# Layer 1 of a mixture of experts on blocks of 768 tokens instead of 384, with its layer 2 right behind, and weight preparation stepping inside layer 1

## The chip, the cores and the metric

The kernel runs on one core of a Trainium2 chip. TensorE (PE) multiplies, VectorE (DVE) and ScalarE (ACT) work on tiles, GpSimd (POOL) does a few special operations, and SyncE (SP) issues nearly all DMAs. The metric is device microseconds of one execution, the median of several runs. Lower is better.

## The reference

Three stages follow one another, all in float32:

```
attention, 4 x 8 heads x 576 positions x 64, window of 64      -> x, 2304 tokens x 512
mixture 1: P = Sinkhorn(softmax(x @ w_gate)), 8 experts
           x1 = sum over e of P[:, e] * (relu(x @ w1[e]) @ w2[e])   (512 -> 1024 -> 512, every token)
mixture 2: each token goes to one expert (capacity 288, greedy by logit)
           out[t] = relu(x1[t] @ v1[e]) @ v2[e]
```

Mixture 1 is dense: each of the eight experts works on all 2304 tokens.

## The kernel before, in words

Each float32 operand is split into two float16 parts, high and low (xh and xl, hh and hl, and so on), and a product is the sum of three matmuls: high by high, high by low, low by high. Partial sums stay in PSUM in float32.

Tokens come in 18 tiles of 128, and TB = 3 tiles make a block of BT = 384 (HB = 192 is half a block, NB = 6 blocks). Expert 0 of mixture 1 is computed beside the attention (line 761). For experts 1 to 7, layer 1 goes by Strassen's scheme (layer1s): the tokens of a block are two halves, the 1024 hidden columns two halves, the 512 inputs two halves, and seven products p1 to p7 take the place of eight. One product is six matmuls of 128 x 192 (line 853). A unit is the seven products for one f of four; it makes hidden chunks f and 4 + f of the block. Some of the operands are combinations of token halves: they are kept as T (th, tl, made by strassen_x) or written over one quarter of x (T1).

ACT copies a product out of PSUM (sa, sb, sc: lines 865, 877, 886), because the next product adds into the same bank; DVE adds the other product; then emit_evac (lines 734, 735) makes hh with a ReLU on ACT and hl on DVE. ACT and DVE take their instructions in order.

Layer 2 (line 931) takes a tile of 128 tokens at a time: 24 matmuls of 512 columns, then one DVE instruction adds the scaled result to acc (line 947). It is a generator that stops four times a tile, so a step is six matmuls.

stream() writes the order of PE's queue by hand. Unit u's products stand at slots 7u + 0, 1, 3, 5, 6, 9, 11; units overlap so that most slots are filled. A free slot takes a step of layer 2: before slot 7 of the block before the last (head), later of the last block (tail). run(e, bs) streams the units of the blocks bs; the first run of an expert has two blocks and no tail. hbuf holds two blocks of hidden values, one per block by turns.

The weights are prepared in the background. weights_all goes through a list of jobs: load 2 MB of float32 weights into raw by four DMAs, scale them by a power of two found from their norm (sum_scale: squares on ACT and DVE, a small matmul with ones on PE at line 293, a few DVE instructions), and split them into high and low. For mixture 2 and for w2 the parts go to DRAM from four small buffers, st2k (ACT line 336, DVE line 338, SP's DMA); for w1 they go to the seven Strassen combinations in SBUF, and this part waits until layer 1 of the expert before is done. bg.tick(level, dt) moves the background's clock on by dt and steps each task that is due and whose level is at least the tick's; a task says how long it wants to wait until its next step. Weights are level 0, as are the last expert's row tiles (finish_all) and gate weights (held_weights). load_w2, which brings the next w2 from DRAM into w2b, is level 1, so it steps at every tick. Layer 2 ticks after each three matmuls (level 0, dt 1). Layer 1 ticks at every third slot, at level 1, dt 2.3. bg.until(name) ticks until a task is done, with no matmul in between.

For the last expert, the last two blocks are held back: their gate logits are computed from the hidden values (held_logits), and the rest of layer 2 runs beside the routing of mixture 2.

Of the kernel before, what the change touches and what calls it, by code (L numbers as in the profile page):

```python
# [172 lines left out]
def body(ctx, tc, q, k, v, wg1, w11, w12, wg2, w21, w22, out):  # L173
# [43 lines left out]
    lg = base.tile([128, NT, E], F32, name="lg")  # L217
    P = base.tile([128, NT, E], F32, name="P")
    SE = base.tile([128, E, NT], F32, name="SE")
    lg2 = base.tile([128, NT, E], F32, name="lg2")  # L220
    lgh = base.tile([128, 2 * TB, E], F32, name="lgh")
    ident = base.tile([128, 128], F32, name="ident")
    wgs = base.tile([128, DC, 2 * E], F16, name="wgs")
    wginv = base.tile([128, 1], F32, name="wginv")
# [51 lines left out]
    def sum_scale(buf, inv, sc, key=None):  # L276


        mp = small.tile([128, 8], F32, name="np8")
        e = []  # L280
        for c in range(0, 8, 2):
            kd = [(key, c // 2)] if key else []
            a = yield Rq("ACT", 0.8, kd, wait=1.3)
            junk = st2k() if "pool" in rc else acc[:, NT - 2].bitcast(F16)
            s0, s1 = [buf[:, x * 512:(x + 1) * 512] for x in (c, c + 1)]
            A.activation(junk[:, 0:512], s0, AF.Square, accum_out=mp[:, c:c + 1])  # L286
            d = yield Rq("DVE", 0.77, kd, wait=0)
            V.scalar_tensor_tensor(junk[:, 512:1024], s1, 1.0, s1, op0=OP.mult, op1=OP.mult, accum_out=mp[:, c + 1:c + 2])
            e += [a.end, d.end]
        m1 = small.tile([128, 1], F32, name="m1")  # L290
        p = yield Rq("PE", 0.2, e, "psb", wait=2.3)
        pt = psb.tile([128, 512], F32, name="pb")
        PE.matmul(pt[:, 0:8], rc["ones"], mp, start=True, stop=True)
        d = yield Rq("DVE", 0.9, [p.end])
        V.tensor_reduce(m1, pt[:, 0:8], AX.X, OP.add)
        norm_pow2(m1, sc, inv)
        fl.release("psb", p.idx, d.start + 0.3)
        rc["sct"] = d.end
# [474 lines left out]
        if i == NT - 1:  # L773
            bg.done.add(("l2x", 0))

    def strassen_x(b):

        c0, c1 = b * BT, b * BT + HB

        def part(x, d, c):  # L780
            return x[:, d:d + 2, c:c + HB]
# [40 lines left out]
        fl.at["T", b] = e  # L822

    def strassen_all():
        for b in range(NB):
            while ("l1b", b) not in bg.done or "T" not in rc or ("lg", b * TB + TB - 1) not in bg.done:
                yield IDLE
            yield from strassen_x(b)
            bg.done.add(("T", b))

    def bq(name, b):
        c0, c1 = b * BT, b * BT + HB
        if name in ("B11", "T1"):
            c = c0 if name == "B11" else c1
            return [x[:, 0:2, c:c + HB] for x in (xh, xl)]
        if name in ("B21", "B22"):
            c = c0 if name == "B21" else c1
            return [x[:, 2:4, c:c + HB] for x in (xh, xl)]
        n = {"T2": 0, "T3": 1, "T4": 2}[name]
        return [t[:, n, :, b * HB:(b + 1) * HB] for t in rc["T"]]  # L840

    def layer1s(e, b):

        hh, hl = hbuf[b % 2]
        sp = rc["spool"]

        def prod(bank, a, x, f, start):
            fs = slice(f * 128, f * 128 + 128)
            aq, xq = wq[a], bq(x, b)
            n = 0  # L850
            for c in range(2):
                for wi, xi in ((0, 0), (0, 1), (1, 0)):
                    PE.matmul(bank[:, 0:HB], aq[wi][:, c, fs], xq[xi][:, c], start=(start and n == 0), stop=(n == 5),  # L853
                              skip_group_check=True)
                    n += 1

        lo, hi = slice(0, HB), slice(HB, BT)
        nf = FC // 2
        s = {}

        def p1(f):
            s["b1", f] = ps1.tile([128, BT], F32, name="p1")
            prod(s["b1", f], "A11", "B11", f, True)
            s["a", f] = sp.tile([128, HB], F32, name="sa")
            A.activation(s["a", f], s["b1", f][:, 0:HB], AF.Copy)

        def p2(f):
            b3 = psb.tile([128, 512], F32, name="pb")
            prod(b3, "A12", "B21", f, True)
            t = s["a", f]  # L870
            V.tensor_tensor(t, b3[:, 0:HB], t, OP.add)  # L871
            emit_evac(hh, hl, f, lo, t)

        def p6(f):
            prod(s["b1", f], "S2", "T2", f, False)
            s["b", f] = sp.tile([128, HB], F32, name="sb")
            A.activation(s["b", f], s["b1", f][:, 0:HB], AF.Copy)  # L877

        def p5(f):
            s["b2", f] = psb.tile([128, 512], F32, name="pb")  # L880
            prod(s["b2", f], "S1", "T1", f, True)

        def p7(f):
            prod(s["b1", f], "S3", "T3", f, False)
            t = s["c", f] = sp.tile([128, HB], F32, name="sc")
            A.activation(t, s["b1", f][:, 0:HB], AF.Copy)  # L886
            V.tensor_tensor(t, s["b2", f][:, 0:HB], t, OP.add)

        def p4(f):
            prod(s["b1", f], "A22", "T4", f, False)  # L890
            emit_evac(hh, hl, nf + f, lo, s["b1", f][:, 0:HB])
            emit_evac(hh, hl, nf + f, hi, s["c", f])

        def p3(f):
            prod(s["b2", f], "S4", "B22", f, False)
            t = s["b", f]
            V.tensor_tensor(t, s["b2", f][:, 0:HB], t, OP.add)  # L897
            emit_evac(hh, hl, f, hi, t)

        return [((0, p1, f), (1, p2, f), (3, p6, f), (5, p5, f), (6, p7, f), (9, p4, f), (11, p3, f)) for f in range(nf)]  # L900

    def stream(units, head, tail):

        at = {}
        for u, unit in enumerate(units):
            for t, fn, f in unit:
                at[7 * u + t] = (fn, f)
        last = max(at)
        for t in range(last + 1):
            if t in at:  # L910
                fn, f = at[t]
                fn(f)
                if t % 3 == 2:
                    bg.tick(1, 2.3)
            else:
                g = head if t < 7 else tail
                if g:
                    next(g, None)
        for _ in head:
            pass  # L920

    def layer2(e, b, out=None):
        hh, hl = hbuf[(1 if b == NB - 2 else 0) if e == 0 else b % 2]
        for j in range(TB):
            i = b * TB + j
            p = ps2.tile([128, DM], F32, name="p2")
            js = slice(j * 128, j * 128 + 128)
            n = 0
            for f in range(FC):
                for h, wi in ((hh, 0), (hh, 1), (hl, 0)):  # L930
                    PE.matmul(p, h[:, f, js], w2v[wi][:, f], start=(n == 0), stop=(n == 3 * FC - 1))  # L931
                    n += 1
                    if n in (3, 6, 9, 12, 15, 18, 21):
                        bg.tick()
                    if n in (6, 12, 18):
                        yield
# [564 lines left out]

    def drain(g, keep=0):

        n = 12 - g[1] - keep
        for _ in range(n):
            next(g[0], None)
        g[1] += n

    def run(e, bs):

        drain(pend[0], 2)
        us = []
        for b in bs:
            us += layer1s(e, b)
        g = [layer2(e, bs[0] - 1), 3] if bs[0] else None
        stream(us, pend[0][0], g and g[0])
        pend[0] = g

    rc["spool"] = mid.enter_context(tc.tile_pool(name="spool", bufs=2))
    for e in range(1, E):  # L1520
        bg.until(("w1", e))
        if e == 1:
            bg.until(("T", 1))
        if e == E - 1:
            bg.start("lgh", held_gate(), 1)
        run(e, [0, 1])
        bg.until(("w2", e), "gates")
        scales(e)
        if e == E - 1:
            bg.start("finish", finish_all())  # L1530
            bg.start("w2h", held_weights())
        pend[0] = [layer2(e, 0), 0]
        for b in range(2, NB):
            if e == 1:
                bg.until(("T", b))
            run(e, [b])
        bg.done.add(("l1", e))
        if e < E - 1:
            drain(pend[0])
            pend[0] = [layer2(e, NB - 1), 0]  # L1540
            drain(pend[0], 3)
            bg.done.add(("l2", e))
    bg.until("weights", "lgh", "w2h")
    mid.close()
    rc["rpool"] = late.enter_context(tc.tile_pool(name="rpool", bufs=1))
# [5 lines left out]

    def rest():
        n = len(finals)
        for g in (pend[0][0], layer2(E - 1, NB - 1)):
            for _ in g:
                while n < len(finals):
                    for _ in to_rows(finals[n], n % 2):
                        pass
                    n += 1


    second()
# [23 lines left out]
```

## Time and profile before

| | |
|---|---|
| median of 3 runs | 1899.92 us (1897.87 to 1900.22) |
| the profiled execution | 1898.91 us |
| its span, first to last instruction | 1897.1 us |
| mean granted clock of PE | 0.987 of full speed |
| layer-1 matmuls of experts 1 to 7, first and last start | 317.4 and 1566.6 us |

The page gives for each engine the time in which it had an instruction running. Matmuls are pipelined, so the length of one matmul (246 ns for 192 columns) says less than the distance from one to the next. A wait is put down to the instruction that released it.

### The profile page before, as it was taken

The page shows a single profiled execution, that of the slowest core. Times are in us where ns is not written, and L with a number is a line of the kernel's source. Part 1 is how long each engine was busy: PE and PEld are TensorE (multiplying, and loading weights), DVE is VectorE, ACT ScalarE, POOL GpSimd, SP SyncE. Part 2 cuts the span into 40 slices and gives each one's busy share as a digit, 9 for nine tenths or more (in the row PEclk, how much of TensorE's full clock was granted, in tenths as well). Part 3 has the DMA queues.
Part 4 walks back from the last instruction along what each step waited for, and adds up shares of the span by engine and source line. Part 5 has one row for each costly group of instructions (what it writes and reads, how often), then busy time and mean ns, then how long its engine had stood idle before and what let it go on. Part 6 is the DMA issues. An engine that isn't in the chain of part 4 may idle for free.

```text
span 1897.1 us, 40554 instructions
## 1 busy us (share of the span) xinstructions
PE 1830.4 (96%) x16103; PEld 1311.0 (69%) x16103; DVE 1235.9 (65%) x3768; ACT 886.0 (47%) x2439; POOL 116.2 (6%) x160
## 2 busy tenths in 40 slices
PE   6999999999999999999999999999999998899987
PEld 5777556767767677667766867667687774677766
DVE  7877955654666766676667666766757767575630
ACT  6776334533555545555554555555534443122222
POOL 0000000000000000000000000000000103233231
PEclk8999999999999999999999999999999999899999
DMA  7663022220333234334252343234231111545360
GB/s 182 124 162 69 13 77 89 90 90 1 112 126 119 90 105 164 115 109 134 90 178 68 112 155 114 95 115 148 90 106 27 36 30 57 187 166 178 123 220 26
DMA packets 172798, 203.38 MB, mean 107 GB/s; under 512 B 83000, under 2 KB 130104, under 8 KB 168512
## 3 DMA queue, kind: packets, MB, share of 16 engines
q1 hardware_dynamic: 164928, 157.78, 27.2%
q0 software_dynamic: 7680, 43.02, 6.5%
q8 instruction: 126, 2.06, 0.4%
q14 instruction: 64, 0.52, 0.1%
HBM read 143.05 MB, written 57.71 MB: 106 GB/s over the span
## 4 chain that ended last, share of the span: by engine, by line
PE 80%; DVE 10%; DMA 4%; ACT 3%; issue 1%; another core or an unknown queue 1%; POOL 0%; SPq 0%; POOLq 0%; ACTq 0%; DVEq 0%
PE p L931 31%; PE p L853 17%; PE pb L853 12%; PE p L1309 4%; PE p L761 4%; PE p L1295 3%; DMA raw<-in_moe_w_dram 1%; PE pb L1140 1%; DVE st2k L338 1%; PE pb L621 1%; DMA w2scr<-st2k 1%; PE pb L608 1%; DVE oh L1221 1%; PE pb L979 1%; DMA ws<-st2k 1%
## 5 line engine op out<-in xcount | busy, mean ns | idle before, releaser
L931 PE MATMUL p<-w2b,hh 128*128 128x512 f16 x2304 | 685.7, 379 | 0.0
L931 PE MATMUL p<-w2b,hl 128*128 128x512 f16 x1152 | 436.6, 379 | 0.0
L931 PEld LDWEIGHTS <-hh 128*128 128x128 f16 x2304 | 221.8, 99 | 217.4
L853 PEld LDWEIGHTS <-w1b 128*128 128x128 f16 x4032 | 340.3, 98 | 23.0 <-issue 4.2
L853 PEld LDWEIGHTS <-w1x 128*128 128x128 f16 x3024 | 256.3, 98 | 19.7 <-issue 5.4
L853 PE MATMUL p<-th,w1x 128*128 128x192 f16 x1344 | 221.2, 246 | 3.6 <-ACT sb L877 2.1
L853 PE MATMUL pb<-xh,w1b 128*128 128x192 f16 x1344 | 221.2, 246 | 0.0
L931 PEld LDWEIGHTS <-hl 128*128 128x128 f16 x1152 | 112.6, 98 | 135.8 <-issue 0.9
L853 PE MATMUL pb<-xl,w1b 128*128 128x192 f16 x672 | 165.3, 246 | 0.0
L853 PE MATMUL p<-tl,w1x 128*128 128x192 f16 x672 | 165.3, 246 | 0.0
L338 DVE SCALAR_TENSOR_TENSOR st2k<-raw,wsc,st2k 128x512 f16<-128x512 f32 x128 | 92.1, 749 | 50.4 <-ACT st2k L336 50.1
L336 ACT ACTIVATE st2k<-raw,wsc 128x512 f16<-128x512 f32 x128 | 86.9, 713 | 69.4 <-DMA ws<-st2k 58.4
L947 DVE SCALAR_TENSOR_TENSOR acc<-p,SE,acc 128x512 f32<-128x512 f32 x126 | 94.0, 746 | 37.1 <-PE p L931 36.7
L734 ACT ACTIVATE hh<-sb 128x192 f16<-128x192 f32 x168 | 61.0, 363 | 112.7 <-DVE sb L897 112.7
L853 PE MATMUL p<-th,w1b 128*128 128x192 f16 x672 | 110.5, 246 | 3.1 <-ACT sc L886 2.9
L734 ACT ACTIVATE hh<-sa 128x192 f16<-128x192 f32 x168 | 60.9, 363 | 107.4 <-DVE sa L871 107.4
L853 PE MATMUL pb<-xh,w1x 128*128 128x192 f16 x672 | 110.6, 246 | 0.0
L853 PE MATMUL p<-xh,w1b 128*128 128x192 f16 x672 | 110.6, 246 | 0.0
L286 ACT ACTIVATE st2k<-raw 128x512 f16<-128x512 f32 x116 | 72.3, 625 | 78.5 <-DMA raw<-in_moe_w_dram 48.0
L996 POOL TENSOR_TENSOR st2k<-tmp,st2k 128x512 f16<-128x512 f32 x18 | 24.4, 1353 | 1372.1 <-ACT tmp L994 1350.8
L871 DVE TENSOR_TENSOR sa<-pb,sa 128x192 f32<-128x192 f32 x168 | 60.0, 357 | 72.7 <-PE pb L853 70.2
L735 DVE SCALAR_TENSOR_TENSOR hl<-sa,hh 128x192 f16<-128x192 f32 x168 | 60.3, 359 | 72.1 <-ACT hh L734 72.1
(303 smaller groups left out, 3245.4 us busy)
## 6 DMA issues: line engine op xcount, KB each, us to landing
raw<-in_moe_w_dram SPq DMA_DIRECT2D x128, 512.0 KB, 5.2
ws<-st2k SPq DMA_DIRECT2D x128, 256.0 KB, 4.5
w2b<-w2scr SPq DMA_DIRECT2D x28, 512.0 KB, 7.3
w2scr<-st2k SPq DMA_DIRECT2D x48, 256.0 KB, 4.6
xrows<-st2k SPq DMA_DIRECT2D x18, 257.0 KB, 3.1
vs<-in_v_dram SPq DMA_DIRECT2D x35, 128.0 KB, 3.5
ldq<-in_q_dram SPq DMA_DIRECT2D x16, 256.0 KB, 4.0
ldk<-in_k_dram SPq DMA_DIRECT2D x16, 256.0 KB, 4.4
```

What stands on the lines that cost most here:

```text
L286: A.activation(junk[:, 0:512], s0, AF.Square, accum_out=mp[:, c:c + 1])
L336: A.activation(hi, src, AF.Copy, scale=sc)
L338: V.scalar_tensor_tensor(lo, src, sc, hi, op0=OP.mult, op1=OP.subtract)
L734: A.activation(hh[:, f, cols], src, AF.Relu)
L735: V.scalar_tensor_tensor(hl[:, f, cols], src, 0.0, hh[:, f, cols], op0=OP.max, op1=OP.subtract)
L761: PE.matmul(p[:, 0:w], w1v[wi][:, c, fs], x[:, c, ts], start=(n == 0), stop=(n == 3 * DC - 1))
L853: PE.matmul(bank[:, 0:HB], aq[wi][:, c, fs], xq[xi][:, c], start=(start and n == 0), stop=(n == 5), skip_group_check=True)
L871: V.tensor_tensor(t, b3[:, 0:HB], t, OP.add)
L931: PE.matmul(p, h[:, f, js], w2v[wi][:, f], start=(n == 0), stop=(n == 3 * FC - 1))
L947: V.scalar_tensor_tensor(acc[:, i], p, SE[:, e, i:i + 1], acc[:, i], op0=OP.mult, op1=OP.add)
L1295: PE.matmul(p[:, 0:CAP], wv1[f // 4][w][:, c, fs], xt[:, x * DC + c], start=(n == 0), stop=(n == 3 * DC - 1))
L1309: PE.matmul(p[:, 0:CAP], wv2[f // 4][w][:, f % 4, dsl], x[:, f], start=(n == 0), stop=(n == 3 * FC - 1))
```

## The change

A block of layer 1 for experts 1 to 7 is now SB = 768 tokens (NS = 3): the two halves of Strassen's scheme are two blocks of 384, so a product is six matmuls of 128 x 384, and the copies and ReLUs of ACT and the DVE operations are 384 wide. The first half writes hbuf[0], the second hbuf[1]. T holds the same amount, in halves of 384. The layer 2 that fills the last free slots of a run, and the stretch behind it, is that of the same block (24 steps, six tiles); it reads hidden chunks 3 and 7 last, which the last unit writes.

Layer 1 ticks after every product, with dt 1.5, at level 0 for even slots and 1 for odd ones. The norm product asks to wait 4.0 instead of 2.3. The copies sa and sc have one buffer instead of two. lg2 and lgh are now views of lg.

```diff
@@ body
+    SB = 2 * BT
+    NS = N // SB
...
-    lg2 = base.tile([128, NT, E], F32, name="lg2")
-    lgh = base.tile([128, 2 * TB, E], F32, name="lgh")
+    lg2 = lg
+    lgh = lg2[:, NT - 2 * TB:]
@@ sum_scale
-        p = yield Rq("PE", 0.2, e, "psb", wait=2.3)
+        p = yield Rq("PE", 0.2, e, "psb", wait=4.0)
@@ strassen_x
-    def strassen_x(b):
-        c0, c1 = b * BT, b * BT + HB
+    def strassen_x(b, part_of):
+        o = part_of * HB
+        c0, c1 = b * SB + o, b * SB + BT + o
...
-        bs = slice(b * HB, (b + 1) * HB)
+        bs = slice(b * BT + o, b * BT + o + HB)
@@ strassen_all
-        for b in range(NB):
-            while ("l1b", b) not in bg.done or "T" not in rc or ("lg", b * TB + TB - 1) not in bg.done:
+        for b in range(NS):
+            while ("l1b", 2 * b + 1) not in bg.done or "T" not in rc or ("lg", (b + 1) * 2 * TB - 1) not in bg.done:
                 yield IDLE
-            yield from strassen_x(b)
+            for x in range(2):
+                yield from strassen_x(b, x)
@@ layer1s
-        hh, hl = hbuf[b % 2]
+        lo, hi = hbuf
...
-                    PE.matmul(bank[:, 0:HB], aq[wi][:, c, fs], xq[xi][:, c], start=(start and n == 0), stop=(n == 5),
+                    PE.matmul(bank[:, 0:BT], aq[wi][:, c, fs], xq[xi][:, c], start=(start and n == 0), stop=(n == 5),
...
-            s["a", f] = sp.tile([128, HB], F32, name="sa")
+            s["a", f] = sp.tile([128, BT], F32, name="sa", bufs=1)
...
-            emit_evac(hh, hl, nf + f, lo, s["b1", f][:, 0:HB])
-            emit_evac(hh, hl, nf + f, hi, s["c", f])
+            emit_evac(*lo, nf + f, every, s["b1", f][:, 0:BT])
+            emit_evac(*hi, nf + f, every, s["c", f])
@@ stream
-                if t % 3 == 2:
-                    bg.tick(1, 2.3)
+                bg.tick(t % 2, 1.5)
@@ layer2
-        hh, hl = hbuf[(1 if b == NB - 2 else 0) if e == 0 else b % 2]
-        for j in range(TB):
-            i = b * TB + j
+        bufs = hbuf if e else [hbuf[1 if b == NB - 2 else 0]]
+        fs = range(FC) if e == 0 else (0, 1, 2, 4, 5, 6, 3, 7)
+        for j in range(TB * len(bufs)):
+            i = b * TB * len(bufs) + j
...
-            for f in range(FC):
+            for f in fs:
@@ the experts
-    def run(e, bs):
-        drain(pend[0], 2)
-        us = []
-        for b in bs:
-            us += layer1s(e, b)
-        g = [layer2(e, bs[0] - 1), 3] if bs[0] else None
-        stream(us, pend[0][0], g and g[0])
-        pend[0] = g
+    def second_layer(e, b):
+        if b == 0:
+            bg.until(("w2", e), "gates")
+            scales(e)
+            if e == E - 1:
+                bg.start("finish", finish_all())
+                bg.start("w2h", held_weights())
+        yield from layer2(e, b)
...
-        run(e, [0, 1])
...
-        for b in range(2, NB):
+        for b in range(NS):
             if e == 1:
                 bg.until(("T", b))
-            run(e, [b])
+            drain(pend[0], 2)
+            us = layer1s(e, b)
+            g = [second_layer(e, b), 3, 24]
+            stream(us, pend[0][0], g[0])
+            pend[0] = g
         bg.done.add(("l1", e))
         if e < E - 1:
-            drain(pend[0])
-            pend[0] = [layer2(e, NB - 1), 0]
-            drain(pend[0], 3)
-            bg.done.add(("l2", e))
+            drain(pend[0], 2)
```

## Rows read from the trace of the kernel before

**Rows 1.** The page, part 1: busy us (share), instructions of each engine.

```profile
PE 1830.4 (96%) x16103; PEld 1311.0 (69%) x16103; DVE 1235.9 (65%) x3768; ACT 886.0 (47%) x2439; POOL 116.2 (6%) x160
```

**Rows 2.** Stretches: length, PE, PEld, DVE, ACT, POOL busy, PE clock, DMA share, GB/s.

```profile
700.00:800.00 100.00, 99.58 (x816) 71.02 (x814) 64.63 (x173) 52.35 (x143) 0.00 (x0) 1.00 0.37 125
1600.00:1700.00 100.00, 85.38 (x941) 63.03 (x941) 63.43 (x250) 21.52 (x43) 27.76 (x28) 0.88 0.47 162
```

**Rows 3.** Line 853, weight loads: count, min/median/max ns, first and last start.

```profile
L853 PEld LDWEIGHTS <-w1b x4032: 95/98/181, 317.2 to 1564.8; 128*128 128x128 f16 x192
L853 PEld LDWEIGHTS <-w1x x3024: 95/98/181, 319.5 to 1566.6; 128*128 128x128 f16 x189
```

**Rows 4.** Timeline of DVE, 512 to 524: start, us, line, operation, [idle before].

```profile
512.61 0.36 DVE L871 TENSOR_TENSOR sa<-pb,sa 128x192 f32<-128x192 f32 x1 [0.34 <-PE pb L853]
...
523.01 0.36 DVE L871 TENSOR_TENSOR sa<-pb,sa 128x192 f32<-128x192 f32 x1 [0.34 <-PE pb L853]
```

**Rows 5.** The chain that ended last, long pieces: start, us, matmuls.

```profile
257.67 15.60 PE p L761 x96
...
828.58 24.61 PE p L931 x114
```

**Rows 6.** Waits of PE: for whom, us in total, times, longest.

```profile
PE p L853 <- ACT sc L886: 2.9, 7, 0.4
PE p L853 <- ACT sb L877: 2.1, 4, 0.7
PE p L853 <- ACT sa L865: 1.3, 2, 0.9
PE pb L293 <- DVE st2k L288: 0.6, 1, 0.6
```

**Rows 7.** Groups of ACT by form: count, busy us, mean ns, idle before.

```profile
L336 ACT ACTIVATE st2k<-raw,wsc 128x512 f16<-128x512 f32 x128 | 86.9, 713 | 69.4 <-DMA ws<-st2k 58.4 <-DVE wsc L307 10.9
L286 ACT ACTIVATE st2k<-raw 128x512 f16<-128x512 f32 x116 | 72.3, 625 | 78.5 <-DMA raw<-in_moe_w_dram 48.0 <-DMA ws<-st2k 20.1 <-DMA w2scr<-st2k 4.4
L741 ACT ACTIVATE hh<-p 128x384 f16<-128x384 f32 x40 | 19.4, 485 | 36.3 <-PE p L761 36.1
```

**Rows 8.** Groups of DVE by form, the same columns.

```profile
L338 DVE SCALAR_TENSOR_TENSOR st2k<-raw,wsc,st2k 128x512 f16<-128x512 f32 x128 | 92.1, 749 | 50.4 <-ACT st2k L336 50.1
L743 DVE SCALAR_TENSOR_TENSOR hl<-p,hh 128x384 f16<-128x384 f32 x40 | 22.1, 554 | 15.9 <-ACT hh L741 15.9
```

**Rows 9.** Timeline of ACT, 808 to 813 us.

```profile
811.53 0.63 ACT L286 ACTIVATE st2k<-raw 128x512 f16<-128x512 f32 x1 [1.04 <-DMA w2scr<-st2k]
...
812.16 0.31 ACT L877 ACTIVATE sb<-p 128x192 f32<-128x192 f32 x1
```

**Rows 10.** The page, part 6: DMA issues, KB each, us to landing.

```profile
raw<-in_moe_w_dram SPq DMA_DIRECT2D x128, 512.0 KB, 5.2
ws<-st2k SPq DMA_DIRECT2D x128, 256.0 KB, 4.5
w2b<-w2scr SPq DMA_DIRECT2D x28, 512.0 KB, 7.3
```

**Rows 11.** Timeline of SP's DMA queue, 499 to 530 us.

```profile
501.71 3.22 SPq L463 DMA_DIRECT2D w2b<-w2scr  x4
529.56 0.56 SPq L422 DMA_DIRECT2D ws<-st2k  x1
```

**Rows 12.** Line 801, the operands T, columns as in rows 3.

```profile
L801 DVE TENSOR_TENSOR tl<-st2k,th x18: 546/553/560, 191.7 to 299.9; 128x384 f16<-128x384 f32 x18
```

**Rows 13.** Timeline of DVE, 1535 to 1600 us.

```profile
1572.14 0.23 DVE L1078 TENSOR_SCALAR tri<-jpr 128x128 f16<-128x128 f32 x1 [2.15 <-POOL jpr L1077]
```

**Rows 14.** Timeline of POOL, 1562 to 1570 us.

```profile
1562.08 0.38 POOL L1023 PARTITION_ALL_REDUCE mm<-m  x1 [9.87 <-DVE m L1021]
1569.78 1.15 POOL L996 TENSOR_TENSOR st2k<-tmp,st2k 128x512 f16<-128x512 f32 x1 [7.32 <-issue]
```

**Rows 15.** Timeline of PE, 1600 to 1612 us.

```profile
1605.57 0.97 PE L1229 MATMUL pb<-rh,oh 128*96 128x6 f16 x18 [1.50 <-DVE rh L1225]
```

More of the change, by code (lines that the diff above doesn't have):

```diff
@@ L821, in strassen_x @@
         fl.release("st2k", i21, e)
-        fl.at["T", b] = e
     def strassen_all():
-        for b in range(NB):
-            while ("l1b", b) not in bg.done or "T" not in rc or ("lg", b * TB + TB - 1) not in bg.done:
+        for b in range(NS):
+            while ("l1b", 2 * b + 1) not in bg.done or "T" not in rc or ("lg", (b + 1) * 2 * TB - 1) not in bg.done:
                 yield IDLE
-            yield from strassen_x(b)
+            for x in range(2):
+                yield from strassen_x(b, x)
             bg.done.add(("T", b))
     def bq(name, b):
-        c0, c1 = b * BT, b * BT + HB
+        c0, c1 = b * SB, b * SB + BT
         if name in ("B11", "T1"):
             c = c0 if name == "B11" else c1
-            return [x[:, 0:2, c:c + HB] for x in (xh, xl)]
+            return [x[:, 0:2, c:c + BT] for x in (xh, xl)]
         if name in ("B21", "B22"):
             c = c0 if name == "B21" else c1
-            return [x[:, 2:4, c:c + HB] for x in (xh, xl)]
+            return [x[:, 2:4, c:c + BT] for x in (xh, xl)]
         n = {"T2": 0, "T3": 1, "T4": 2}[name]
-        return [t[:, n, :, b * HB:(b + 1) * HB] for t in rc["T"]]
+        return [t[:, n, :, b * BT:(b + 1) * BT] for t in rc["T"]]
     def layer1s(e, b):
-        hh, hl = hbuf[b % 2]
+        lo, hi = hbuf
         sp = rc["spool"]
@@ L852, in prod @@
                 for wi, xi in ((0, 0), (0, 1), (1, 0)):
-                    PE.matmul(bank[:, 0:HB], aq[wi][:, c, fs], xq[xi][:, c], start=(start and n == 0), stop=(n == 5),
+                    PE.matmul(bank[:, 0:BT], aq[wi][:, c, fs], xq[xi][:, c], start=(start and n == 0), stop=(n == 5),
                               skip_group_check=True)
                     n += 1
-        lo, hi = slice(0, HB), slice(HB, BT)
+        every = slice(0, BT)
         nf = FC // 2
@@ L863, in p1 @@
             prod(s["b1", f], "A11", "B11", f, True)
-            s["a", f] = sp.tile([128, HB], F32, name="sa")
-            A.activation(s["a", f], s["b1", f][:, 0:HB], AF.Copy)
+            s["a", f] = sp.tile([128, BT], F32, name="sa", bufs=1)
+            A.activation(s["a", f], s["b1", f][:, 0:BT], AF.Copy)
         def p2(f):
@@ L870, in p2 @@
             t = s["a", f]
-            V.tensor_tensor(t, b3[:, 0:HB], t, OP.add)
-            emit_evac(hh, hl, f, lo, t)
+            V.tensor_tensor(t, b3[:, 0:BT], t, OP.add)
+            emit_evac(*lo, f, every, t)
         def p6(f):
             prod(s["b1", f], "S2", "T2", f, False)
-            s["b", f] = sp.tile([128, HB], F32, name="sb")
-            A.activation(s["b", f], s["b1", f][:, 0:HB], AF.Copy)
+            s["b", f] = sp.tile([128, BT], F32, name="sb")
+            A.activation(s["b", f], s["b1", f][:, 0:BT], AF.Copy)
         def p5(f):
@@ L884, in p7 @@
             prod(s["b1", f], "S3", "T3", f, False)
-            t = s["c", f] = sp.tile([128, HB], F32, name="sc")
-            A.activation(t, s["b1", f][:, 0:HB], AF.Copy)
-            V.tensor_tensor(t, s["b2", f][:, 0:HB], t, OP.add)
+            t = s["c", f] = sp.tile([128, BT], F32, name="sc", bufs=1)
+            A.activation(t, s["b1", f][:, 0:BT], AF.Copy)
+            V.tensor_tensor(t, s["b2", f][:, 0:BT], t, OP.add)
         def p4(f):
             prod(s["b1", f], "A22", "T4", f, False)
-            emit_evac(hh, hl, nf + f, lo, s["b1", f][:, 0:HB])
-            emit_evac(hh, hl, nf + f, hi, s["c", f])
+            emit_evac(*lo, nf + f, every, s["b1", f][:, 0:BT])
+            emit_evac(*hi, nf + f, every, s["c", f])
         def p3(f):
@@ L896, in p3 @@
             t = s["b", f]
-            V.tensor_tensor(t, s["b2", f][:, 0:HB], t, OP.add)
-            emit_evac(hh, hl, f, hi, t)
+            V.tensor_tensor(t, s["b2", f][:, 0:BT], t, OP.add)
+            emit_evac(*hi, f, every, t)
         return [((0, p1, f), (1, p2, f), (3, p6, f), (5, p5, f), (6, p7, f), (9, p4, f), (11, p3, f)) for f in range(nf)]
@@ L922, in layer2 @@
     def layer2(e, b, out=None):
-        hh, hl = hbuf[(1 if b == NB - 2 else 0) if e == 0 else b % 2]
-        for j in range(TB):
-            i = b * TB + j
+        bufs = hbuf if e else [hbuf[1 if b == NB - 2 else 0]]
+        fs = range(FC) if e == 0 else (0, 1, 2, 4, 5, 6, 3, 7)
+        for j in range(TB * len(bufs)):
+            i = b * TB * len(bufs) + j
             p = ps2.tile([128, DM], F32, name="p2")
-            js = slice(j * 128, j * 128 + 128)
+            hh, hl = bufs[j // TB]
+            js = slice(j % TB * 128, j % TB * 128 + 128)
             n = 0
-            for f in range(FC):
+            for f in fs:
                 for h, wi in ((hh, 0), (hh, 1), (hl, 0)):
@@ L1502, in drain @@
     def drain(g, keep=0):
-        n = 12 - g[1] - keep
+        n = g[2] - g[1] - keep
         for _ in range(n):
@@ L1507, in drain @@
         g[1] += n
-    def run(e, bs):
-        drain(pend[0], 2)
-        us = []
-        for b in bs:
-            us += layer1s(e, b)
-        g = [layer2(e, bs[0] - 1), 3] if bs[0] else None
-        stream(us, pend[0][0], g and g[0])
-        pend[0] = g
+    pend[0].append(12)
+    def second_layer(e, b):
[6 more added lines that the diff above has]
+        yield from layer2(e, b)
     rc["spool"] = mid.enter_context(tc.tile_pool(name="spool", bufs=2))
@@ L1521, in body @@
         bg.until(("w1", e))
-        if e == 1:
-            bg.until(("T", 1))
         if e == E - 1:
             bg.start("lgh", held_gate(), 1)
-        run(e, [0, 1])
[L1527 to L1532, printed above, removed]
-        for b in range(2, NB):
+        for b in range(NS):
             if e == 1:
                 bg.until(("T", b))
-            run(e, [b])
+            drain(pend[0], 2)
[3 more added lines that the diff above has]
+            pend[0] = g
         bg.done.add(("l1", e))
         if e < E - 1:
-            drain(pend[0])
-            pend[0] = [layer2(e, NB - 1), 0]
-            drain(pend[0], 3)
-            bg.done.add(("l2", e))
+            drain(pend[0], 2)
     bg.until("weights", "lgh", "w2h")
@@ L1553, in rest @@
         n = len(finals)
[L1554 to L1559, printed above, removed]
+        for _ in pend[0][0]:
+            while n < len(finals):
+                for _ in to_rows(finals[n], n % 2):
+                    pass
+                n += 1
     second()
```

## The prediction, made before the change was run

> **What bounds the kernel now.** I read the page's busy times first: TensorE (PE) is busy 1830.4 of 1897.1 us, no other engine over 65% [rows 1]. An average hides stages, so next came the busy time by stretch of 100 us: where the change lies (experts 1 to 7, 317 to 1567 us) PE is busy nearly all the time (99.6% from 700 to 800) at a granted clock of 1.00; only after 1600 does it fall, to 85% [rows 2, 3]. So in the changed stage the end is set by how many microseconds of matmul stand in PE's queue, plus the few that PE spends parked. The waits of PE show the second part: in the whole layer 1 it waited 6.3 us, for ACT's copies out of PSUM, and 0.6 us for a norm product [rows 6]. The reader is to see two small levers: the length of PE's own stream, and about 7 us of waits that can shrink or grow.
>
> **PE's stream.** The groups of weight loads give 4032 + 3024 = 7056 layer-1 matmuls of 192 columns in seven experts [rows 3]. One unit of 42 of them passes every 3.467 us: DVE's add of "sa" comes once a unit, at 512.61 and, three units later, at 523.01, so 10.40 us / 126 = 82.5 ns each [rows 4]. After the change there are half as many at 384 columns. The trace has that shape in expert 0: 96 in 15.60 us, 162.5 ns each [rows 5]. 7056 x 82.5 = 582.1 us becomes 3528 x 162.5 = 573.3: about 9 us less (8.8; the pitches are good to 0.1 ns, so 8 to 10). Layer 2 keeps its 432 matmuls an expert at 215.9 ns (24.61 us / 114) [rows 5], in another order of f.
>
> The Trainium skill (TensorE: Matmul & The Clock Gate, section "Back-to-back issue gap") gives a sustained 81 ns at 128 and 131 ns at 512 columns for streams of weight load and matmul. By that an estimate for 384 would be near 114 ns and the change would save over 200 us; the trace has 215.9 ns at 512 columns, so the rule doesn't hold here and I give it no chance.
>
> **Waits that go.** Seven waits for "sc", 0.42 us each, 2.9 in all [rows 6]: one an expert. In the first run of an expert the last unit has no layer 2 to fill its free slots, so p4 follows p7 at once. Now layer 2 of the same block fills them in every run: -2.9. The other three sorts (sb 2.1, sa 1.3, norm 0.6: 4.0 us) come where ACT is held by weight steps at a seam of layer 2 and layer 1: at 811.53 a background square had waited 1.04 us for a store to free its buffer, the copy "sb" came behind it at 812.16, and this is the longest of the sb waits, 0.7 us [rows 6, 9]. These seams are rearranged; I count the old ones out, -4.0, and the new ones in, next.
>
> **Weight steps inside layer 1.** The tick there was on level 1, which weight preparation (level 0) ignores; now every slot with an even t is a level-0 tick. A product lasts 6 x 0.1625 = 0.975 us, so a step (one 512-wide ACT pass, 0.713 us, one DVE pass, 0.749) may come every 1.95 us. A unit has besides seven ACT operations of 0.485 and seven DVE operations of 0.554 [rows 7, 8], 3.4 and 3.9 us of 6.83; with 3.5 steps 5.9 and 6.5 us. That fits, but tightly, and both queues are in order, so it can be late without being full. By hand, from the start of an even p1: product done 1.0; copy sa 1.2 to 1.65; weight split on ACT to 2.35, on DVE to 3.1; only then the add for p2 (to 3.6), its ReLU on ACT (to 4.1), the two ReLUs of p4 (to 5.1), the next split (to 5.8), and the copy sb that p6 had ready at 4.1 ends at 6.2. p7, which adds into the same bank, is due at 5.85: 0.35 us of wait, 0.5 with no overlap. With one of the steps left out it is in time. Steps run in about two of three blocks of experts 2 to 6 (five jobs of some 15 steps an expert), less in expert 1, and in expert 7 row tiles and the gate's weights take their place (a row tile holds ACT for a square and two 512-wide passes with a DVE chain between, some 3 us): 53 of 84 units. Bounds: the nearest row, the sb and sa waits of before (3.4 us over about 300 level-0 ticks at the seams), gives 2 us for some 200 ticks; 0.5 in every unit gives 26. I take 0.12 a unit, +6.4, near the lower end because each product now gives twice the time and the ACT operations are only half as long again.
>
> **Queues that the steps move past.** Their DMAs, all on SP's queue, move too. The four loads of w2b are issued early in an expert's first run, 501.71 to 504.9; the next weight store came 25 us later, when layer 1 was over [rows 11]. Now stores and the next 512 KB loads go out right behind them. A store takes 4.5 us to land, a w2b load 7.3, a raw load 5.2 [rows 10]; four buffers at a step per 1.95 us give 7.8 us, against 0.71 + 0.75 + 0.6 + 4.5 = 6.6 us for one. A store 3 to 4 us later holds ACT some 2 to 3 us once an expert, and PE by what exceeds the slack of about 1.4: 0 to 1.5 us, taken as 0.5 in six experts, +3. w2b itself is hidden: about 22 us from its issue to slot 28, where layer 2 first reads it.
>
> **Norm products.** PE waits there for the last of eight squares, with all of layer 2 queued behind it. Before, the pause of layer 1 lay between a job's splits and its norm, so only one of them waited. Now the next job's squares follow at once; the product gets 1.7 units more (1.1 us of layer 2). Bounds: nothing, or what ACT's squares have waited for raw and stores, 72.5 us in 116 [rows 7], about 2.5 us a job, less those 1.1: 1.4 us in 17 jobs (three of five an expert), 24 us. I take +2, near the old 0.6.
>
> **Parts taken at nothing.** The operands T are finished by 299.9, before the first layer-1 product at 317.2 [rows 3, 12]; a two-part wait there still has cover, and without it would cost a part's 10 us. The shared lg and lgh hold no operation. One copy of sa and sc instead of two: each has four or five slots (4 to 5 us) till its next use. Layer 2 reading f 3 and 7 last leaves 2.9 us between p4's product and its reader; two ACT and two DVE passes take 2.1.
>
> **The end.** DVE waits 2.15 us at 1572.14 for constants from POOL, which had stood 7.32 us after the all-reduce of the gate's weights at 1562.08; later PE waits for DVE, 1.50 us at 1605.57 for one [rows 13 to 15]. With ticks inside layer 1 that all-reduce comes before the last block: 0 to -2.2, taken as -1.5.
>
> **The sum**, on the profiled execution (1898.91 us, 1.0 under the median of 1899.92; its span 1897.1 and 1.8 around it): -8.8 - 2.9 - 4.0 + 6.4 + 3.0 + 2.0 - 1.5 = -5.8, so 1893.1, predicted as **1893**. The likeliest case by itself reaches from 1888 to 1896.
>
> **Rivals.**
> *The norm products take over the wait.* The weight jobs lose their pause. In layer 2 a split is asked for every 2.2 units (a unit is three matmuls, 0.65 us), 1.42 us, and the four buffers let one pass per 6.6 / 4 = 1.65: after eight, with its own 1.46, DVE is some 3.3 us behind PE's place. The raw piece loaded behind it lands 0.6 + 5.2 us on, its square ends at 9.7, and the norm product stands at 9 + 4 units, 8.4 us: PE is parked 1.3 us, less where a job's splits lie in layer 1, say 1 us in 17 jobs: 17 us, 15 more than I took: **1908**. For it: ACT's waits on DMA are long [rows 7]. Against: only one such wait before. It decides from 0.46 us a job, where (5.8 + 2.0) / 17 is used up.
> *Layer 1 pays for its steps.* The handworked late copy in most units: 0.24 x 53 = 12.7, 6.3 more than taken: **1899**, no change.
> *All of it hides.* New waits of 3 us in all instead of 11.4: **1885**.
> *The change doesn't do what it says:* the steps could find no work in layer 1; then waits shrink and this is the case before, so it has no time of its own.
>
> **Chances.** Forecast 0.34, all hidden 0.15, no change 0.23, norm waits 0.28. A run of this kernel can tell 0.2%, 3.8 us, from none: faster (under 1896.1) 0.34 + 0.14 = 0.48; within 0.24; slower (over 1903.7) 0.28. The range must take in both signs: 1884 to 1908.
>
> **What would show it.** 3528 matmuls of 128x384 at 162 ns a piece; no "sc" wait. Waits of PE on sa, sb, sc of 5 to 12 us in layer 1 prove the step cost; the wait of the norm products, under 4 us or near 17, decides between forecast and first rival. DVE's wait for POOL's constants is gone or not. Wrong would be: an expert's period (317.2 to 1566.7 over seven, 178.5 us [rows 3]) that doesn't fall although these waits stay small, or w2b late.

## The result, and the profile after

The change made the kernel slower: a median of 1924.9 us in 4 runs (1923.8 to 1926.5) against 1900.1 for the kernel before on the same chip, ratio 1.0131 with a 95% interval of 1.0118 to 1.0145. The forecast was 1893, with a range to 1908. The profiled run took 1924.7 us, its span 1922.9, 25.8 more than before.

The page of the changed kernel, part 1, answers to [rows 1], and the stretches (length, busy PE, PEld, DVE, ACT, POOL, granted PE clock, DMA share, GB/s) to [rows 2]:

```profile
PE 1832.5 (95%) x12575; PEld 1075.1 (56%) x12575; DVE 1170.1 (61%) x3180; ACT 801.8 (42%) x1851; POOL 116.4 (6%) x160
```

```profile
500.00:600.00 100.00, 95.65 (x516) 50.72 (x514) 68.15 (x144) 54.27 (x118) 0.00 (x0) 0.98 0.59 190
700.00:800.00 100.00, 96.92 (x508) 49.52 (x508) 64.24 (x140) 45.92 (x101) 0.00 (x0) 1.00 0.43 143
1600.00:1700.00 100.00, 83.32 (x855) 55.49 (x854) 67.55 (x275) 22.98 (x46) 28.57 (x27) 0.88 0.39 141
```

PE's busy time is 2.1 us over that of [rows 1], though its layer-1 products have become some 10 us shorter: part of it now runs at a lower clock. From 700 to 800 it is 2.7 us under [rows 2]. The weight loads of layer 1 answer to [rows 3], the waits of PE between 319 and 1590 us (total, times, longest) to [rows 6]:

```profile
L856 PEld LDWEIGHTS <-w1b x2016: 95/98/181, 318.8 to 1587.7; 128*128 128x128 f16 x184
L856 PEld LDWEIGHTS <-w1x x1512: 95/98/181, 322.0 to 1589.9; 128*128 128x128 f16 x189
```

```profile
PE p L856 <- ACT sb L880: 16.5, 5, 3.9
PE pb L978 <- DVE acc L951: 5.0, 4, 3.2
PE pb L295 <- DVE st2k L290: 4.3, 9, 1.2
PE pb L295 <- ACT st2k L288: 3.5, 7, 0.8
```

There are half as many products and no wait for "sc", as forecast. But PE parks 16.5 us for "sb" in five waits, one in each of experts 2 to 6; 7.8 us at the norm products (0.6 before); 5.0 us for acc in expert 7 (1.4 before).

**One of the five.** The timeline of PE (start, us, operation, idle before), then the same stretch with its clock:

```profile
516.05 0.33 PE L856 MATMUL pb<-xh,w1b 128*128 128x384 f16 x1
519.63 0.32 PE L856 MATMUL p<-th,w1x 128*128 128x384 f16 x1 [3.26 <-ACT sb L880]
519.80 0.32 PE L856 MATMUL p<-tl,w1x 128*128 128x384 f16 x1
...
520.91 0.53 PE L856 MATMUL p<-xl,w1b 128*128 128x384 f16 x1
521.23 0.85 PE L856 MATMUL p<-xh,w1b 128*128 128x384 f16 x2
...
524.07 0.33 PE L856 MATMUL pb<-xh,w1b 128*128 128x384 f16 x1
```

```profile
516.30:519.60 3.30, 0.08 (x1) 0.00 (x0) 2.71 (x6) 2.30 (x5) 0.00 (x0) 1.00 0.88 332
519.60:520.60 1.00, 0.96 (x6) 0.58 (x6) 0.86 (x2) 0.11 (x1) 0.00 (x0) 1.00 0.03 11
520.60:524.00 3.40, 3.40 (x13) 1.65 (x11) 1.63 (x4) 1.90 (x5) 0.00 (x0) 0.50 0.82 231
```

PE stands 3.26 us, runs 1 us at full speed, and then the granted clock is 0.50 (the 1.2 GHz level) until 524.0: matmuls start 0.32 us apart instead of 0.16. So the wait is paid about one and a half times. ACT's timeline shows what was late, SP's queue why:

```profile
511.96 0.48 ACT L868 ACTIVATE sa<-p 128x384 f32<-128x384 f32 x1
515.27 0.72 ACT L338 ACTIVATE st2k<-raw,wsc 128x512 f16<-128x512 f32 x1 [2.83 <-DMA ws<-st2k]
517.28 0.52 ACT L736 ACTIVATE hh<-sa 128x384 f16<-128x384 f32 x1 [1.28 <-DVE sa L874]
...
518.49 0.71 ACT L338 ACTIVATE st2k<-raw,wsc 128x512 f16<-128x512 f32 x1
519.11 0.48 ACT L880 ACTIVATE sb<-p 128x384 f32<-128x384 f32 x1
```

```profile
503.64 2.74 SPq L465 DMA_DIRECT2D w2b<-w2scr  x4
506.48 2.38 SPq L424 DMA_DIRECT2D ws<-st2k  x2
```

The buffer that ACT wants at 512.4 was split at 504.13 and finished by DVE at 505.62. Its store is issued only at 506.48, when SP is through with the four w2b loads, and lands 8.8 us later, the longest landing of such a store from 500 to 525 us, against a median of 4.0 us for such stores over the stage. DVE's add to "sa" is queued behind the other half of that split (it starts at 516.70), ACT's ReLU waits for it, and "sb" ends 3.3 us late.

### The profile page after: what moved, and what is told of

It reads as the page before. It is cut to its first block, busy times and chain, and to the rows that moved or that the text cites. A ratio compares the mean times of both kernels' runs of the same rounds, so it can differ in the third digit from the quotient of the medians.

```text
span 1922.9 us, 32199 instructions
## 1 busy us (share of the span) xinstructions
PE 1832.5 (95%) x12575; PEld 1075.1 (56%) x12575; DVE 1170.1 (61%) x3180; ACT 801.8 (42%) x1851; POOL 116.4 (6%) x160
## 5 line engine op out<-in xcount | busy, mean ns | idle before, releaser
L856 PEld LDWEIGHTS <-w1b 128*128 128x128 f16 x2016 | 199.5, 99 | 139.1 <-issue 7.1
L856 PEld LDWEIGHTS <-w1x 128*128 128x128 f16 x1512 | 148.7, 99 | 119.3 <-issue 19.7
L856 PE MATMUL p<-th,w1x 128*128 128x384 f16 x672 | 193.4, 329 | 16.5 <-ACT sb L880 16.5
L856 PE MATMUL pb<-xh,w1b 128*128 128x384 f16 x672 | 193.2, 329 | 0.0
L856 PE MATMUL p<-tl,w1x 128*128 128x384 f16 x336 | 110.7, 329 | 0.0
L856 PE MATMUL pb<-xl,w1b 128*128 128x384 f16 x336 | 110.7, 329 | 0.0
L288 ACT ACTIVATE st2k<-raw 128x512 f16<-128x512 f32 x116 | 72.4, 625 | 85.8 <-DMA raw<-in_moe_w_dram 71.2
L763 PE MATMUL p<-xh,w1b 128*128 128x384 f16 (+1 forms) x512 | 100.7, 289 | 7.4 <-DVE hl L745 6.0
L856 PE MATMUL p<-xh,w1b 128*128 128x384 f16 x336 | 98.3, 334 | 0.0
L856 PE MATMUL p<-th,w1b 128*128 128x384 f16 x336 | 95.6, 326 | 0.0
L856 PE MATMUL pb<-xh,w1x 128*128 128x384 f16 x336 | 95.6, 326 | 0.0
```

The lines of the kernel that those rows point to most:

```text
L763: PE.matmul(p[:, 0:w], w1v[wi][:, c, fs], x[:, c, ts], start=(n == 0), stop=(n == 3 * DC - 1))
L856: PE.matmul(bank[:, 0:BT], aq[wi][:, c, fs], xq[xi][:, c], start=(start and n == 0), stop=(n == 5), skip_group_check=True)
```

## Where the 25.8 us lie

I added up PE's start-to-start times from the first layer-1 product to the last layer-2 product, and took the idle time out. That stage grew from 1286.3 to 1308.1 us. Layer 1's own time went from 584.7 to 582.7, all other matmuls' from 691.3 to 694.4, idle time from 10.3 to 31.0. The rest is 1.6 us ahead of the stage and 2.4 behind it; it isn't explained here. The kernel before has no half-rate stretch in its stage, and the first kernel below has one alone, behind a wait for acc in expert 7: there layer 1's own time is 574.1. So the half rate costs the changed kernel 8.6 us in layer 1, and the block change by itself saves 10.6.

## The experiments

My theory after this: the store behind w2b, passed on to PE because ACT has no slack where it strikes, and made dearer by the clock. The rival: ACT and DVE are too full with weight steps in layer 1, and the store is beside the point. Times are ratios to the kernel before on the same chip; the chips of the three groups differ, above all in the tail after layer 2, which is 282 to 285 us in the profiles of the two held kernels, of the norm product at 2.3 and of the last edit, and 289 to 296 in the others, so across groups I compare the stage.

### Spread the w2b loads

```
         SP.dma_start(w2b2[:, :, rs], w2rows(e)[:, :, rs])
+        yield 6
```

> Edit to the changed kernel: the four 512 KB loads of w2b go out one every four layer-1 slots (3.9 us) instead of back to back. Theory 'store behind w2b': the four sb waits of 2.8 to 3.9 us come because one weight store lands late behind 2 MB of w2b; spread, a store meets at most one load, ACT is no longer held, the sb waits fall from 16.5 us to under 3, the granted clock stays at 1.00 behind them, and the time falls by 16.5 + 8.4 (half-rate matmuls) = 25 us, to 1898 to 1905. Rival 'ACT and DVE are too full': the store is beside the point, the sb waits stay over 10 us and the time over 1915.

Measured: 1900.4 us, ratio 1.0014 (1.0000 to 1.0028). PE's waits, 319 to 1590 us:

```profile
PE pb L979 <- DVE acc L952: 4.4, 3, 3.4
PE pb L295 <- DVE st2k L290: 3.5, 8, 1.1
PE pb L295 <- ACT st2k L288: 3.2, 5, 1.3
PE p L857 <- ACT sb L881: 1.6, 5, 0.3
```

The sb waits fall from 16.5 to 1.6 us, as the theory said, and the stage from 1308.1 to 1286.2. What stays of sb, 0.31 us in each of five experts, is the handworked lateness of the prediction (0.35): with steps running, "sb" has no slack there at all, but only once an expert. A store still took 7.5 us to land (513.95 to 521.43), but ACT waited for none from 500 to 530: what counts is when the buffer is wanted.

### Issue them from another queue

```
-        SP.dma_start(w2b2[:, :, rs], w2rows(e)[:, :, rs])
+        G.dma_start(w2b2[:, :, rs], w2rows(e)[:, :, rs])
```

> Edit: the four w2b loads are issued by POOL's queue, still back to back; everything else as in the changed kernel. If the order of one queue holds the store (it is issued behind the four loads on SP), its landing goes back from 8.8 us to 4 to 5 and the sb waits to under 3 us: 1898 to 1905. If the shared DMA engines hold it, it still lands after some 8 us, the sb waits stay over 10 us, and the time stays within 1915 to 1925.

Measured: 1900.3 us, ratio 1.0010 (1.0000 to 1.0020); sb waits:

```profile
PE p L856 <- ACT sb L880: 4.6, 5, 1.9
```

The time is in the first range, but the longest landing of a store, 7.4 us, is nearer the 8 of the second case, and the sb waits are over the first's 3 us. The loads issued by POOL, then the late store by SP:

```profile
494.18 0.72 POOL L465 DMA_DIRECT2D w2b<-w2scr  x1 [168.99 <-PE p L935]
500.47 2.16 POOL L465 DMA_DIRECT2D w2b<-w2scr  x3 [5.58 <-PE p L935]
504.72 3.16 SPq L424 DMA_DIRECT2D ws<-st2k  x2
```

The loads no longer went out back to back: counted from the start of the same split on ACT (504.13 in the changed kernel, 503.19 here), the first went 8.5 us sooner and the others 2.8. ACT's wait for the store fell from 2.83 to 0.60 us. Of these 2.2 us, 0.8 is the store's earlier issue, its place in the queue, and 1.4 its shorter landing (7.4 us for 8.8); whether the other queue or the earlier loads shortened it is not shown. The Trainium skill (DMA: Bandwidth & Descriptors, section "Issuing engines are not separate DMA queues") says that DMAs of all issuing engines interleave on the same 16 engines, and that starting them from several saves the issue time only, which is usually small. The landing of 7.4 us beside another queue's loads agrees with that, and so do the 0.8 us. That the sb waits fell by 12 us is the effect of the whole edit.

### No weight step in layer 1

```
-                bg.tick(t % 2, 1.5)
+                bg.tick(1, 1.5)
```

> Edit: no weight step in layer 1 (its tick is back on level 1), the 768-token blocks kept. Both theories: no sb wait over 1 us, granted clock 1.00, norm waits back under 2 us. What is left is the block change alone: 9 us of matmul and 2.9 us of sc waits less than before, so 1885 to 1895, if layer 2 alone still has room for the steps; if it hasn't, PE waits at each expert's start for the last splits (waits of layer 1 on w1b from DVE or ACT), 5 us or more in six experts, and the time is over 1915.

Measured: 1900.6 us, ratio 1.0009 (1.0000 to 1.0019). It lies between the two cases. No sb wait is left, but layer 2 alone has not quite the room for the steps:

```profile
PE p L856 <- DVE w1b L340: 10.2, 3, 3.8
PE pb L295 <- ACT st2k L288: 3.2, 6, 0.8
PE pb L978 <- DVE acc L951: 0.3, 1, 0.3
```

Three experts (not six) start with PE waiting for their last splits, 10.2 us, and the half rate behind it costs 3.7 (577.8 against 574.1). The acc waits of expert 7 are gone with its steps. So steps in layer 1 are needed, at a lower price than they had.

### A step in every third slot

```
-                bg.tick(t % 2, 1.5)
+                bg.tick(0 if t % 3 == 2 else 1, 1.5)
```

> Edit: a weight step in every third layer-1 slot (2.93 us) instead of every second. Theory 'store behind w2b': four buffers then come round in 11.7 us, over the 8.8 us that the late store took, so the sb waits fall under 3 us and the time to 1897 to 1905. Rival 'too full': the waits shrink with the rate, 16.5 x 2/3 = 11 us, and the time to about 1915.

Measured: 1906.9 us, ratio 1.0049 (1.0032 to 1.0065). The stall is gone, as the theory had it (1.5 us of "sc" waits in its place), but the time is over its range: the norm products now wait 12.3 us (10.5 for ACT's squares, 1.8 for DVE's) and acc 6.3. I think that fewer slots push the jobs together in layer 2; no run tests that by itself. It speaks for the store (the rival had 11 us of sb waits), but the forecast of the time missed.

### Steps in layer 1 with the old blocks

```
-                if t % 3 == 2:
-                    bg.tick(1, 2.3)
+                if t % 2 == 1:
+                    bg.tick(t // 2 % 2, 1.5)
```

> Edit to the kernel before: weight steps also inside layer 1, one per four slots (1.98 us, as often as in the changed kernel), with 384-token blocks. If the store behind w2b alone makes the stall, the old blocks show it too: an sb, sa or sc wait of 2 to 4 us in each of experts 2 to 6 and a granted clock under 1.00 behind it, 1912 to 1925. If it needs the larger blocks' fuller ACT and DVE, the waits stay under 1 us each and the time within 1895 to 1902.

Measured: 2002.3 us, ratio 1.0545 (1.0520 to 1.0570). Both expected times miss by 77 us or more. PE's waits:

```profile
PE p L853 <- ACT sb L877: 41.2, 60, 4.6
PE p L853 <- ACT sc L886: 22.0, 28, 3.4
```

The waits of the first expectation are there, though: in each of experts 2 to 6 one sb wait of 3.3 to 4.6 us, 18.6 in all, four of them with half rate behind. In expert 2 a store, issued at 511.12 right behind the four w2b loads, lands 8.75 us later, and ACT stands for it, then PE:

```profile
519.89 0.72 ACT L336 ACTIVATE st2k<-raw,wsc 128x512 f16<-128x512 f32 x1 [2.37 <-DMA ws<-st2k]
522.80 0.24 PE L853 MATMUL p<-th,w1x 128*128 128x192 f16 x1 [3.31 <-ACT sb L877]
```

So the stall behind w2b doesn't need the larger blocks. The dozens of other waits are what neither case had. With 384 tokens a product lasts half as long, but a copy out of PSUM takes 0.31 us [rows 9] against 0.48 for twice the columns (the ACT rows above), and there are twice as many. At one step in four slots, an estimate from this run's mean times (seven operations of 0.34 us and 1.75 splits of 0.71 on ACT, seven of 0.35 and 1.75 of 0.75 on DVE) gives 3.6 and 3.8 us in each unit of 3.47: the rival's "too full" fits the old blocks, where for the larger ones the prediction had 5.9 and 6.5 of 6.83. That is a sum, not a test of its own.

### Hold ACT by a known time

Base: the kernel with spread loads. Seven experts, once each, at the place where the store had struck; the other kernel has 7 for 3.

```
         V.tensor_tensor(t, b3[:, 0:BT], t, OP.add)
+        for _ in range(3 if b == 0 and f == 2 else 0):
+            A.activation(lo[0][:, f, every], t, AF.Relu)
         emit_evac(*lo, f, every, t)
```

> Edit to the kernel with spread w2b loads (1900.4 us): in block 0 of each expert, unit 2, ACT does the ReLU of sa three times more, some 1.3 us of ACT time where the late store had held it 2.83. Theory 'no slack': sb is already 0.31 us late there, so PE parks 0.3 + 1.3 = 1.6 us in experts 2 to 6 (less in 1 and 7, which run no weight steps there), short enough for the clock: +6 to +8 us, 1906 to 1908. Rival, the slack of 1.4 us in the prediction: the waits stay at 0.3 us and the time at 1900 to 1901.

> Edit: as the one with three, but seven ReLU passes more, some 2.9 us. Theory 'no slack' with the clock: PE parks 3.2 us in experts 2 to 6 and 1 to 3 us in 1 and 7, and after most of these the granted clock falls as it did after the 2.8 to 3.9 us waits: 16 + 4 + 8 = 28 us more than the spread kernel, 1922 to 1930. Without the effect on the clock: 1918 to 1922. With 1.4 us of slack: 2.9 - 1.4 in seven experts, 1909 to 1912.

Measured: ratios 1.0095 (1.0072 to 1.0118) and 1.0227 (1.0210 to 1.0244), 1905.7 and 1928.6 us where the kernel before took 1886.8. PE's wait for "sb" in expert 2, with three and with seven:

```profile
520.50 0.32 PE L857 MATMUL p<-th,w1x 128*128 128x384 f16 x1 [1.97 <-ACT sb L883]
```

```profile
525.54 0.48 PE L857 MATMUL p<-th,w1x 128*128 128x384 f16 x1 [4.19 <-ACT sb L883]
```

(4.19 - 1.97) / 4 is 0.55 us a pass, as on ACT (1.63 us for three, 3.85 for seven), and 0.32 + 3 x 0.55 gives 1.97: each microsecond of ACT is a microsecond of PE, from the first on. The slack of 1.4 us is refuted. The sums were missed: the stage is 13.9 and 39.8 us longer than with spread loads, where 6 to 8 and 28 were expected, since I had priced a pass at 0.42 and taken 2 us as too short for the clock. With three passes two of the six waits were followed by a half-rate stretch in layer 1; this is the one in expert 2:

```profile
521.30:524.70 3.40, 3.40 (x13) 1.65 (x11) 1.71 (x5) 2.11 (x5) 0.00 (x0) 0.50 0.95 244
```

Layer 1's own time is 577.6 with three and 589.8 with seven passes, against 574.1: 3.5 and 15.7 us of half rate, for 11.4 and 24.7 us of waits.

### Move the norm product both ways

Base: spread loads.

```
-        p = yield Rq("PE", 0.2, e, "psb", wait=4.0)
+        p = yield Rq("PE", 0.2, e, "psb", wait=8.0)
```

> Edit: the spread w2b loads, and the norm product is asked for 8.0 instead of 4.0 step units after its squares. Theory 'squares late': PE parks there because the next job's squares wait for their 512 KB of raw, up to 1.3 us a job, 6.7 us in all and 8.1 with the pipeline refill; 2.6 us more of layer 2 cover them. Waits under 1.5 us, time 6 to 8 us under the kernel with spread loads alone, 1892 to 1895. If a later product only makes the splits behind it late, the splits' buffers or the seam of the next expert show new waits of as much, and the time stays at 1900.

> Edit: spread w2b loads, and the norm product back where it stood before the change (2.3 units after the squares). Theory 'squares late': it comes 1.7 units, 1.1 us, earlier, so the thirteen waits grow by up to 1.1 us each and others begin: PE's waits there go from 6.7 to 18 to 25 us and the time to 1912 to 1920. If the position doesn't matter, 1900.

Measured at 8.0: 1889.2 us, ratio 0.9947 (0.9934 to 0.9961), faster than before and under the range expected. At 2.3, the old place: ratio 1.0112 (1.0087 to 1.0136), 1908.8 us where the kernel before took 1886.8; its 20.5 us of waits are those expected. PE's waits at 8.0 have no norm product left:

```profile
PE pb L979 <- DVE acc L952: 5.6, 4, 3.4
PE p L857 <- ACT sb L881: 1.6, 5, 0.3
PE pb L1210 <- DVE tot L1207: 0.6, 1, 0.6
```

and at 2.3 they are the largest item:

```profile
PE pb L295 <- ACT st2k L288: 14.3, 9, 2.1
PE pb L295 <- DVE st2k L290: 6.2, 9, 1.0
```

The stage took 1302.7, 1286.2 and 1272.7 us with the product at 2.3, 4.0 and 8.0. The 6.7 us of waits at 4.0 are less than the 13.5 between them and 8.0: beside them the matmuls' own time falls by 6.6 (661.8 to 657.3 in layer 2, 35.2 to 33.1 in the small ones). Some 2.8 of that, by estimate, is chance: at 4.0 half rate followed a wait for acc of 3.44 us in expert 7, at 8.0 none followed one of 3.42. The other 3.8 I put to what restarts had cost. No new wait of the splits came. What makes the squares late shows in the page of the changed kernel: ACT's waited 71.2 us for their pieces of raw, where [rows 7] had 48.0.

```profile
L288 ACT ACTIVATE st2k<-raw 128x512 f16<-128x512 f32 x116 | 72.4, 625 | 85.8 <-DMA raw<-in_moe_w_dram 71.2
```

### The gate's constants in expert 7

```
         G.partition_all_reduce(mm, m1, 128, bass.bass_isa.ReduceOp.max)
-        yield 3
+        yield 13
```

> Edit: the spread w2b loads, and DVE is asked for the gate constants 13 instead of 3 step units after POOL's all-reduce. Theory: in expert 7 DVE stands 6.1 us for POOL with the adds to acc behind it, and PE parks 3.4 us for acc; with 6.5 us more in between the wait is gone, and the few half-rate matmuls behind it: time 4 to 6 us under the spread loads alone, 1894 to 1897. Rival: the transposes wait for the adds anyway (0.5 us twice before that place); then 1 us at most.

> Edit: all three together (spread w2b loads, norm product at 8.0, gate constants at 13). If the three causes are all there is between the changed kernel and the block change by itself, the layer-1 matmuls save 9, sc 2.9, sb and sa 3, and the new waits are under 3 us: 1886 to 1890, 9 to 12 us faster than before. If something else holds it (the end, the plan of expert 0), it stays over 1893.

Measured: 1903.0 us, ratio 1.0021 (1.0012 to 1.0030), with spread loads; 1891.2, ratio 0.9955 (0.9942 to 0.9969), with the norm product at 8.0 as well. Both are over their ranges, and the three edits are no faster than spread loads and the norm product alone (ratio 0.9947). The first theory falls: the wait for acc didn't go, its longest grew from 3.4 to 5.5 us. POOL's timeline of the kernel with all three edits, then DVE's:

```profile
1500.75 1.16 POOL L1001 TENSOR_TENSOR st2k<-tmp,st2k 128x512 f16<-128x512 f32 x1 [4.91 <-ACT tmp L999]
1508.82 0.38 POOL L1028 PARTITION_ALL_REDUCE mm<-m  x1 [6.91 <-issue]
1516.34 1.14 POOL L1001 TENSOR_TENSOR st2k<-tmp,st2k 128x512 f16<-128x512 f32 x1 [7.15 <-issue]
```

```profile
1518.27 0.15 DVE L305 TENSOR_SCALAR pbn<-x2m 128x1 int32<-128x1 int32 x1 [6.94 <-ACT tmp L991]
...
1519.18 0.74 DVE L952 SCALAR_TENSOR_TENSOR acc<-p,SE,acc 128x512 f32<-128x512 f32 x1
```

POOL stands 6.9 us ahead of the all-reduce and 7.2 behind it, waiting for nothing that the profile shows. A row tile's subtraction is queued behind; its source buffer is ACT's next square's target, DVE's scale waits for that square, and the add to acc comes behind it. Asking DVE later only changed which of the two it stood for. That gave the last edit, to all three: take POOL out of the row tiles.

```
-        G.tensor_tensor(xr[:, DM:2 * DM], xs, xr[:, 0:DM], OP.subtract)
+        V.tensor_tensor(xr[:, DM:2 * DM], xs, xr[:, 0:DM], OP.subtract)
```

> Edit: spread loads, norm product at 8.0, gate constants at 13, and the low halves of the row tiles subtracted by DVE instead of POOL. Theory 'POOL stands some 14 us around its all-reduce': the row tile queued behind it held ACT's next square and by that the add to acc; with POOL out of that chain the wait for acc (3.4 to 5.6 us) is under 1 us, and the time 4 to 6 us under the kernel with three edits: 1883 to 1887. Rival: the subtractions make DVE late at the end and the time stays at 1889 to 1892.

Measured: ratio 0.9909 (0.9893 to 0.9926), 1869.7 us where the kernel before took 1886.8: the fastest of all, 17 us under before. That is 8 to 9 us beyond what the three edits gave, over the 4 to 6 expected. Its stage takes 1266.5 us, 9.6 less than with three edits (and 19.8 less than before). POOL and PE's waits:

```profile
1502.63 0.35 POOL L1028 PARTITION_ALL_REDUCE mm<-m  x1 [1310.35 <-DVE m L1026]
```

```profile
PE p L857 <- ACT sb L881: 1.6, 5, 0.3
PE pb L1234 <- DVE rh L1230: 1.5, 1, 1.5
PE pb L979 <- DVE acc L952: 1.0, 2, 0.5
```

The all-reduce starts at once, when DVE's maximum is there, and the waits for acc are 1.0 us where the three edits had 6.6.

## Why the prediction was wrong, by its steps

- **PE's stream, -8.8.** Right: layer 1's own time fell by 10.6 us where no clock hid it.
- **Waits that go, -2.9 and -4.0.** Right: no wait for sa or sc is left, and sb's old places are gone.
- **Weight steps inside layer 1, +6.4.** Priced too high: 1.6 us with spread loads. The hand-drawn schedule was right to 0.04 us, but such a place comes once an expert, not in 53 units.
- **Queues that the steps move past, +3.0. This step failed.** The mechanism was the right one, store behind w2b, ACT held 2 to 3 us (2.83). The price was not: sb waits of 16.5 - 1.6 = 14.9 us and 8.6 of half rate, 23.5 in all. Two errors: a slack of about 1.4 us was assumed, though the paragraph before had worked out a place with none (the held kernels show none there); and a parked PE was priced at its own length, though [rows 2] showed a granted clock of 0.88 where PE had gaps.
- **Norm products, +2.0.** Too low, and the first rival (15 us more) was nearer: 7.8 us of waits, and 3.1 more in the other matmuls' own time, which I put to restarts. It named late squares, and ACT's do wait longer for raw; that the missing pause between jobs is the reason was not tested by itself. Here the change's own 1.7 units helped: without them the stage is 16.5 us longer.
- **The end, -1.5.** Wrong in sign. DVE's wait for POOL's constants is gone, as forecast, but PE's waits for "rh" behind it are not (4.6 us before, 5.4 after). The all-reduce did come earlier, but into expert 7's row tiles, where POOL's standing reached PE through ACT, DVE and acc: 3.6 us more of waits.
- **The range.** It reached 1908, the norm rival by itself. That several rivals come true together, and that the w2b collision, bounded at 1.5 us an expert, costs 4.7, was in no case.

Against the sum of -5.8: steps -4.8, collision +20.5, norm products +8.9, end +5.1, stream -1.8, and +4.0 ahead of and behind the stage: 31.9, beside the 31.6 us between it and the 25.8 measured.

## What to carry to other kernels

When background work moves into a stage, draw the in-order queues at the fullest place and take the slack from there; a DMA that holds one ACT instruction is then paid by PE in full, and the clock may add half of it again. Large loads that nobody needs soon go out one by one between the small stores on whose buffers an engine turns. Before a wait is moved, follow the chain to what really stands: postponing DVE's question left POOL where it was.

## What the runs showed of the hardware

- **Short stops and the clock.** In the changed kernel, sb waits of 2.75 to 3.92 us were followed by a granted clock of 0.50 in four of five cases (not the one of 2.76 at 702.29). In the held kernels, sb waits of 1.56 to 1.98 us were followed by it in two of six, those of 3.78 to 4.19 us in all six. Of the longest acc wait of each larger-block kernel in expert 7, where it was over 3 us, those of 3.19 (the changed kernel) and 3.42 us (norm product at 8.0) were not, eight of 3.44 to 5.81 us were. The fall came during the stop or up to 1.1 us after PE had started again. So in these runs the length of a stop alone doesn't tell whether the clock falls.
- **POOL's change of operation.** Between a tensor_tensor and the all-reduce POOL stood 6.0 to 6.9 us, and 6.7 to 7.3 us on the way back ([rows 14] has 7.32); with no tensor_tensor on POOL, its last operation another all-reduce, it started 0.1 us after DVE's maximum.
- **DVE beside POOL.** DVE's scale of the gate weights (128x64 float32) took 1.09 us in nine kernels, where a tensor_tensor of POOL ran beside it, and 0.25 us in the four where POOL ran nothing beside it.
- **Pitch at 384 columns** is 162.5 ns in layer 1 too, as in expert 0 [rows 5].
